# Decayed attention and a sticky mixture of experts on one core: where the transposed groups of q and k get their bank, who copies them, and the order of the last queries' value products

## The chip, the cores and the metric

The kernel runs on one core of a Trainium2 chip. The metric is the device time of one execution in microseconds. The engines are named as the profile names them: PE (TensorE, with PEld for its weight loads), DVE (VectorE), ACT (ScalarE), POOL (GpSimd) and SP (SyncE, which here only issues DMAs). PSUM is the memory that PE writes its products to; the kernel uses it in banks of 128 x 512 float32.

## The reference

q, k and v have 8 batches, 8 heads, 576 positions and 64 columns; f has a decay factor per position. Causal attention with a decay is followed by a layer of 8 experts, of which each token uses one:

```python
scores = scale * q @ k.T                       # per batch and head, 576 x 576
cum = cumsum(log(clip(f, 1e-4, 1)))
scores = where(causal, -1e9, scores + cum[:, None] - cum[None, :])
attn = softmax(scores)
x = attn @ v                                   # heads side by side: [8, 576, 512]

logits = x @ w_gate;  local = sigmoid(x @ w_local)
for s in range(576):                           # per batch, in order
    fresh = argmax(logits[s])
    e = fresh if s == 0 or local[s] < 0.5 else prev_e
    prev_e = e
    out[s] = softmax(logits[s])[e] * (relu(x[s] @ w1[e]) @ w2[e])
```

w1 is 8 x 512 x 1024 and w2 is 8 x 1024 x 512.

## The kernel before

**Number format.** Every float32 factor is split in two float16 parts, a high and a low one, and a product is made of three float16 products (high with high, high with low, low with high).

**Attention.** For each batch b there are 25 units. Twenty of them have 128 queries: per pair of heads j two "c" units, two "a" units and one "b" unit. The 576 positions leave 64 queries over, and these are the last-query units: four of them (`d1unit`, lines 958 to 995) take the last 64 queries of two heads against the first 512 keys, one head on PSUM partitions 0 to 63 and the other on 64 to 127, and a fifth (`d2unit`, lines 997 to 1006) takes them against the last 64 keys for all eight heads.

A unit goes through stages: `sc` scores into a bank "st" (PE, line 863), `mx` the negative maximum (DVE, line 874), `ex` the exponential (ACT, line 891), `tr` the transpose of the result into a bank "pt" (PE, line 906), `hi` its high part (ACT, line 911), `lo` the low part as a difference (DVE, line 915), and `av` the value products (PE, line 885) into a bank "xp". Some units take another way to the low part: `sub` subtracts on PE (line 918) and `lo2` copies on ACT (line 923). `SUBS` (line 30) lists these units. `n1` and `n2` (DVE, lines 946 and 950) divide by the sums. In `av` each block has three products: high weights with high and low values, low weights with high values. A last-query unit has 24 products with 64 stationary columns; all twelve of one half come before the twelve of the other.

**Banks.** PSUM has four banks "st", two "pt" and two "xp" (lines 115 to 117).

**q and k of the next batch.** While batch b runs, `prep(b + 1)` (line 484) hands work to POOL: high and low parts of q, then k, then v. From b = 2 on q and k are then turned (`prep_turned`, line 420) in groups of eight 128 x 128 blocks, five groups for each (the fifth has four): `tq` is eight transposes on PE (line 447) into a bank "pt", `eq` the copy out of it, on ACT for q (lines 454 and 457, with the scale) and on DVE for k (line 452). After the second, fourth and fifth group a DMA issued by SP carries the high parts to a second copy, QB or KB (lines 366 and 373), which the second half of every score needs. There are two copies of these in turn, so the next batch's can be written while the present one is read.

**Order.** The order of instructions on each engine is fixed when the program is written. A planner (`issue`, line 1204) keeps a list of units for each stage and clocks for the engines, estimates when each candidate could start, and takes the one with the lowest start plus the weight `W` of its stage; equal ones are ranked by `RANK` (lines 1125 to 1127). A stage also needs room among its banks. Groups of q and k come into the lists in `add_turns` (line 1234), as soon as POOL's part has been handed out, before each unit's `step`. Scores of the next batch wait, in the planner's reckoning, for the groups that they need (line 1115).

**Side work.** The gate of batch b - 1 and, after every second batch, the routing of two batches (which expert, which slot) are a chain of small steps that the planner mixes in as stage "side". They are put in at unit `GI` of the batch (lines 42 and 1731): 21 in batch 1, 16 in the later ones. Routing steps run on DVE and partly on POOL, those of the third pair of batches, which fall into the last batch, on DVE alone. `early_idx` and `early_tok` (lines 1699 and 1703) at the end of that chain fetch the first three tiles of expert 0's tokens from the first six batches, so that expert 0 can start as soon as the attention ends.

**Experts.** Lines 1650 and 1664 are the products of the experts; the last pair's routing runs beside the first three tiles.

Of the kernel before, what the change touches and what calls it, by code (L numbers as in the profile page):

```python
# [26 lines left out]
ROUND = 1.5 * 2.0 ** 30  # L27
CAP = 5
EARLY = 3
SUBS = (3, 5, 8, 16, 18)  # L30


def moves_of(d):
# [5 lines left out]
ORDA = moves_of("q0:P k:M 0:V 1:V k:ag")  # L39
ORDB = moves_of("q:ag q0:T 2:V q1:P k0:P k1:P q:e k:e 3:V q1:T q:Tl k0:T :vl :Vl q:2 q:C 0:K k1:T :iv v0:P k:2 1:K")  # L40

GI = (21, 16, 16)
LI = (14, 18)
PX = 6
XI = 3

UO = tuple(range(25))
NP = 0
# [15 lines left out]
def kernel(  # L64
# [355 lines left out]
    def prep_turned(b, nm):  # L420

        def begin():
            if line["eq"]:
                issue((line["eq"][-1][0], "eq"))
            new_prep(b, nm)
            prep_aug(b, nm)

        def half(g0, g1):
            R = {}

            def parts(i):
                t, t16 = LT[b, nm], Tq[b][nm + "t"]
                if not R:
                    hi, lo = (t16[:, :, 0:64], t16[:, :, 64:128]) if nm == "q" else (t16[:, :, 64:128], t16[:, :, 0:64])
                    R["p"] = hi_lo(hi[:, g0:g1], lo[:, g0:g1], t[:, g0:g1], (g1 - g0) // 2)
                R["p"][i][1]()

            return [(64 * (g1 - g0), lambda i=i: parts(i)) for i in range(3)]

        def group(j):  # L440
            U = {}

            def tq():
                t16 = Tq[b][nm + "t"]
                U["pt"] = psT.tile([128, 8, 128], F16, name="pt")
                for a in range(4 if j == 4 else 8):
                    nc.tensor.transpose(U["pt"][:, a], t16[:, 8 * j + a], ident16)  # L447

            def eq():
                A, pt = Tq[b][nm + "A"], U["pt"]  # L450
                if nm == "k":
                    nc.vector.tensor_copy(flat(A[:, 8 * j:min(8 * j + 8, 36)]), flat(pt[:, 0:4 if j == 4 else 8]))
                elif j == 4:
                    nc.scalar.activation(flat(A[:, 32:36]), flat(pt[:, 0:4]), AF.Copy, scale=SCALE)
                else:
                    dst = flat(A[:, 0:32]).rearrange("p (c g x) -> p g c x", c=2, x=64)[:, 8 * j:8 * j + 8]
                    nc.scalar.activation(dst, pt.rearrange("p g (c x) -> p g c x", c=2), AF.Copy, scale=SCALE)
                if j in (1, 3):
                    copy_hi(b, nm, 2 * j - 2, 2 * j + 2)
                elif j == 4:  # L460
                    copy_last(b, nm)

            c = 0.5 if j == 4 else 1.0
            eng, cost = ("ACT", 130 + 880 * c) if nm == "q" else ("DVE", 100 + 570 * c)
            return {"key": (b, nm, j), "tq": ("PE", 460 * c, tq, {"psT": 1}, {}), "eq": (eng, cost, eq, {}, {"psT": 1})}

        def ready(js):
            return (0, lambda: turns.extend(group(j) for j in js))

        return [(0, begin)] + half(0, 16) + [ready((0, 1))] + half(16, 36) + [ready((2, 3, 4))]  # L470
# [358 lines left out]
    def compute(b, T):  # L829
# [48 lines left out]
            nc.tensor.matmul(xo[:, :, 64], lhsT=eps[:, 0:128], rhs=eps[:, 128:128 + xo.shape[1]], start=True, stop=False,  # L878
                             skip_group_check=True)

        def av(xo, ph, pl, blks):
            n = len(blks)
            for i, (c0, m, vi) in enumerate(blks):
                for jj, (a, w) in enumerate(((ph, vh), (ph, vl), (pl, vh))):
                    nc.tensor.matmul(xo, lhsT=a[:, c0:c0 + m], rhs=w[:, vi, :],  # L885
                                     start=False, stop=(i == n - 1 and jj == 2),
                                     skip_group_check=True)

        def expo(P, st, c0, c1, bias):

# [67 lines left out]
        def d1unit(j):  # L958
            c = 32 + j

            def sc():
                if j == 0:
                    d2 = X["d2"] = psS.tile([128, 512], F32, name="st")
                    scores(d2, [(4 * r + jj, 4, (4,), r * 64, jj * 64, jj == 0) for jj in range(4) for r in range(2)])
                    for jj in range(4):
                        nc.tensor.matmul(d2[:, jj * 64:(jj + 1) * 64], lhsT=mA2, rhs=mB2,
                                         start=False, stop=True, skip_group_check=True)
                    X["P2"] = work.tile([128, 256], F32, name="P2", bufs=1)
                st = X["d", j] = psS.tile([128, 512], F32, name="st")
                scores(st, [(4 * r + j, 4, ORD4, r * 64, 0, True) for r in range(2)])  # L970

            def mx():
                if j == 0:
                    negmax(nm[:, 40:44], X["d2"][:, 0:256].rearrange("p (j x) -> p j x", j=4))
                negmax(nm[:, 44:45], X["d", j])

            def mn():
                nc.vector.tensor_tensor(nm[:, c:c + 1], nm[:, 44:45], nm[:, 40 + j:41 + j], ALU.min)

            def ex(P):  # L980
                expo(P, X["d", j], 0, 512, nm[:, c:c + 1])
                nc.scalar.activation(X["P2"][:, j * 64:(j + 1) * 64], X["d2"][:, j * 64:(j + 1) * 64], AF.Exp,
                                     bias=nm[:, c:c + 1])

            def avf(ph, pl):
                if j == 0:
                    X["xd"] = psX.tile([128, 4, 65], F32, name="xp")
                    guard(X["xd"])
                for r in range(2):
                    av(X["xd"][r * 64:(r + 1) * 64, j, :], ph, pl,  # L990
                       [(i * 128 + r * 64, 64, c * 8 + 4 * r + j) for i, c in enumerate(ORD4)])

            unit(sc, mx, ex, avf, (1020 if j == 0 else 478, 930 if j == 0 else 598, 769, 705 if j == 0 else 680), takes=1 + (j == 0),
                 frees=1 + (j == 3), first=j == 0)
            units[-1]["mn"] = "DVE", 69, mn, {}, {}

        def d2unit():
            def avf(ph, pl):
                for j in range(4):
                    g, u = j // 2, j % 2  # L1000
                    for r in range(2):
                        av(X["xd"][r * 64:(r + 1) * 64, j, :], ph, pl,
                           [(g * 128 + r * 64, 64, 32 + 4 * u + 2 * r + g)])

            unit(nop, nop, None, avf, (0, 0, 0, 680), cols=256, src=lambda: X["P2"])
            norm(lambda: X["xd"], xnl, [128, 4])

        def aunit(j, r):
# [17 lines left out]
            def avf(ph, pl):  # L1026
                if r == 0:
                    X["xp", j] = psX.tile([128, 6, 65], F32, name="xp")
                    guard(X["xp", j])
                xp = X["xp", j]  # L1030
                av(xp[:, r, :], ph, pl, [(0, 128, h)])
                av(xp[:, 4 + r, :], ph, pl, [(128 + i * 128, 128, c * 8 + h) for i, c in enumerate(ORD3)])

            unit(sc, mx, ex, avf, (545, 663, 715, 360 + 25 * (r == 0)), first=r == 0)

        def bunit(j):
# [11 lines left out]

            def avf(ph, pl):
                for r in range(2):  # L1050
                    av(X["xp", j][:, 2 + r, :], ph, pl,
                       [(r * 256 + i * 128, 128, i * 8 + 2 * j + r) for i in range(2)])

            unit(sc, mx, ex, avf, (543, 598, 716, 360))
            norm(lambda: X["xp", j].rearrange("p (c r) x -> p c r x", r=2),
# [2 lines left out]
        def cunit(j, r):  # L1058
# [13 lines left out]
            def avf(ph, pl):  # L1072
                if r == 0:
                    X["xc", j] = psX.tile([128, 2, 65], F32, name="xp")
                    guard(X["xc", j])
                av(X["xc", j][:, r, :], ph, pl, [(i * 128, 128, c * 8 + h) for i, c in enumerate(ORD4)])

            unit(sc, mx, ex, avf, (488, 598, 571, 360 + 25 * (r == 0)), first=r == 0)
            if r == 1:
# [42 lines left out]
    STAGES = ("sc", "mx", "mn", "ex", "tr", "hi", "lo", "sub", "lo2", "av", "n1", "n2", "tq", "eq")  # L1122
    RANK = {st: 0.0 for st in STAGES + ("side",)}
    RANK["side"] = -20
    RANK.update({'sc': 8.2, 'mx': 13.1, 'mn': -16.4, 'ex': 24.2, 'tr': -17.4, 'hi': 3.9, 'lo': 8.2, 'sub': -2.5, 'lo2': -6.1, 'av': 12.7, 'n1': -11.4, 'n2': -7.3, 'side': -52.7, 'tq': 30.0, 'eq': -10.0})
    W = {st: 0 for st in RANK}
    W.update({'sc': -70, 'mx': -60, 'mn': -270, 'ex': 270, 'tr': -130, 'hi': -40, 'lo': -150, 'sub': -140, 'lo2': 0, 'av': -40, 'n1': -180, 'n2': -110, 'side': -180, 'tq': 0, 'eq': -100})
    clock = {"PE": T0, "ACT": T0, "DVE": T0, "POOL": T0}
    due = deque()
    pools = {}  # L1130
# [45 lines left out]
    def side_next():  # L1176
        eng, cost = COSTS.get(chain[0].__name__, ("DVE", 160))
        after = [side["end"]]
        if chain[0].__name__ in OPENS and side["run"] is None:
            if not room["psS"]:  # L1180
                return None, eng, cost
# [49 lines left out]
    turned = {}  # L1231
    count = [0]

    def add_turns():
        while turns:
            u = turns.popleft()
            u["ready"] = clock["POOL"]
            n = serial[0] - 0.5 + 1e-4 * count[0]
            count[0] += 1
# [467 lines left out]
    for b in range(B):  # L1707
# [3 lines left out]
        for i, u in enumerate(units):  # L1711
# [4 lines left out]
            if not due:  # L1716
                if b < B - 1 or i < XP:
                    pump((23 if b == B - 1 else 25) - i)
                ship(i if i < 24 else 99)
                add_turns()  # L1720
            step(u)
            if b == B - 1:
                if i == 5:
# [3 lines left out]
                    ectx = ExitStack()  # L1727
                    ep = ectx.enter_context(tc.tile_pool(name="ep", bufs=1, side="right"))
                    W0 = wtiles(wpa)
                    queue.extend(early_weights(stage, W0, range(6)))  # L1730
            if b > 0 and i == GI[(b > 1) + (b >= B - 2)]:
                for j, x in enumerate(gate(b - 1)):
# [299 lines left out]
```

## Time and profile before

| | |
|---|---|
| median of 3 timed runs | 951.12 us (948.55 to 955.56) |
| profiled execution | 944.52 us, its span 942.8 us |
| mean granted PE clock in it | 0.965 |
| attention ends, first expert product | about 457 us, 459.48 us |
| a batch in the middle of the attention | 53 to 56 us, 25 units |
| last batch | 393 to 457 us |

A line of the profile's groups or of its order in time names the engine, the line of the kernel, the operation, the tiles out<-in with their shapes, the count and the duration; in square brackets or behind the last bar stands the idle time of the engine just before it and what ended it. A line of a stretch has its length, then the busy time of PE, PEld, DVE, ACT and POOL with the number of instructions, then the granted PE clock, the DMA engines' busy share and GB/s. An "x2" in the order of time joins two instructions that started together or one right behind the other.

### The profile page before, as it was taken

To read this page: it belongs to the slowest core of one execution; us is meant where nothing else is said; L and a number is where in the kernel's file an instruction comes from. 1 tells how busy PE (TensorE), PEld (TensorE's weight loads), DVE (VectorE), ACT (ScalarE), POOL (GpSimd) and SP (SyncE) were. 2 spreads that over 40 slices of the span, in tenths; PEclk is the share of its full clock that TensorE was granted. 3 is DMA by queue.
4 is the path that set the end of the run, shared out by engine and by line. 5 is a ranking of instruction groups with operands and counts; after the bars stand their busy time and mean duration, and the time that the engine had idled before them with its cause. 6 is when DMAs were issued, how large, how long until landed. Compare 5 with 4: busy or idle time off the path is not lost.

```text
span 942.8 us, 21055 instructions
## 1 busy us (share of the span) xinstructions
PE 832.2 (88%) x8566; PEld 571.5 (61%) x8566; DVE 530.1 (56%) x1109; ACT 425.2 (45%) x795; POOL 417.4 (44%) x479
## 2 busy tenths in 40 slices
PE   5697989889898889878886998799999999999993
PEld 3575777677776777666644664465647465655651
DVE  7584777777687767897563586433414243433200
ACT  5685868487785858566322322131312323131110
POOL 9685985395836957156632204213040312333020
PEclk9898999999999999998998999899999999999997
DMA  7989968355756644174637639936272837332010
GB/s 171 197 158 208 193 125 184 83 123 128 167 126 137 158 102 105 38 194 114 154 111 200 189 96 251 267 78 198 87 224 94 221 120 190 123 90 87 1 42 6
DMA packets 210243, 130.58 MB, mean 138 GB/s; under 512 B 149054, under 2 KB 185024, under 8 KB 210060
## 3 DMA queue, kind: packets, MB, share of 16 engines
q1 hardware_dynamic: 202369, 104.83, 48.6%
q0 software_dynamic: 7776, 24.39, 7.9%
q8 instruction: 68, 1.11, 0.5%
q14 instruction: 30, 0.25, 0.1%
HBM read 77.39 MB, written 20.41 MB: 104 GB/s over the span
## 4 chain that ended last, share of the span: by engine, by line
PE 64%; DVE 11%; DMA 9%; ACT 5%; POOL 4%; issue 4%; SPq 2%; POOLq 0%; DVEq 0%; ACTq 0%
PE z L1650 20%; PE y L1664 18%; PE pt L906 7%; PE st L863 7%; PE xp L885 6%; DVE pl L915 2%; DMA stg<-in_moe_w_dram 2%; DVE nm L874 2%; ACT P L891 2%; DMA KB<-Ak 2%; ACT ph L911 1%; DMA out_dram<-o,xs 1%; POOL xr L305 1%; PE pt L447 1%; PE st L870 1%
## 5 line engine op out<-in xcount | busy, mean ns | idle before, releaser
L1650 PE MATMUL z<-xT,wh 128*128 128x320 f16 (+3 forms) x1088 | 193.4, 298 | 18.4 <-DVE hl L1637 17.9
L891 ACT ACTIVATE P<-st,nm 128x512 f32<-128x512 f32 (+3 forms) x288 | 152.0, 584 | 60.9 <-DVE nm L874 56.5
L874 DVE TENSOR_REDUCE nm<-st 128x1 f32<-128x512 f32 (+4 forms) x264 | 133.8, 544 | 41.1 <-PE st L870 35.0
L1650 PEld LDWEIGHTS <-wh 128*128 128x128 f16 x1088 | 105.7, 99 | 61.2 <-issue 16.7
L906 PE MATMUL pt<-ident,P 128*128 128x128 f32 x784 | 123.4, 285 | 21.8 <-DVE pl L915 11.7
L911 ACT CAST ph<-pt 128x512 f16<-128x512 f32 (+1 forms) x200 | 114.5, 582 | 48.3 <-PE pt L906 43.3
L1618 POOL DMA_INDIRECT xg<-xs,mg x37 | 44.0, 1188 | 194.1 <-DMA xT<-xg 164.5
L1664 PE MATMUL y<-uh,hh 128*128 128x512 f16 x328 | 125.0, 381 | 3.7 <-ACT o L1641 3.7
L915 DVE TENSOR_TENSOR pl<-pt,ph 128x512 f16<-128x512 f32 (+1 forms) x160 | 106.5, 670 | 36.7 <-ACT ph L911 33.4
L1664 PE MATMUL y<-ul,hh 128*128 128x512 f16 x328 | 125.0, 381 | 0.0
L1664 PE MATMUL y<-uh,hl 128*128 128x512 f16 x328 | 124.8, 381 | 0.0
L1650 PE MATMUL z<-xT,wl 128*128 128x320 f16 (+3 forms) x544 | 123.7, 297 | 0.0
L1636 ACT ACTIVATE hh<-z 128x640 f16<-128x640 f32 (+3 forms) x80 | 48.4, 607 | 164.5 <-PE z L1650 155.3
L1637 DVE SCALAR_TENSOR_TENSOR hl<-z,hh 128x640 f16<-128x640 f32 (+3 forms) x80 | 55.8, 701 | 113.2 <-ACT hh L1636 113.2
L1664 PEld LDWEIGHTS <-hh 128*128 128x128 f16 x656 | 64.2, 98 | 79.3 <-issue 5.3
L906 PEld LDWEIGHTS pt<-ident,P 128*128 128x128 f32 x784 | 86.0, 144 | 34.7 <-ACT pl L923 8.4
L885 PE MATMUL xp<-VH,pl 128*128 128x65 f16 (+1 forms) x960 | 99.4, 195 | 3.1 <-DVE pl L915 1.9
L885 PE MATMUL xp<-VH,ph 128*128 128x65 f16 (+1 forms) x960 | 101.5, 198 | 0.1
L885 PE MATMUL xp<-VL,ph 128*128 128x65 f16 (+1 forms) x960 | 100.3, 196 | 0.0
L885 PEld LDWEIGHTS <-ph 128*128 128x128 f16 (+1 forms) x1920 | 91.6, 103 | 14.2 <-issue 10.3
L863 PE MATMUL st<-KB,QB 70*128 70x256 f16 (+4 forms) x448 | 81.0, 290 | 14.8 <-DMA KB<-Ak 14.8
L1642 POOL DMA_INDIRECT out_dram<-o,ms x37 | 40.1, 1085 | 109.1 <-ACT o L1641 64.9
(345 smaller groups left out, 1315.7 us busy)
## 6 DMA issues: line engine op xcount, KB each, us to landing
stg<-in_moe_w_dram SPq DMA_DIRECT2D x64, 512.0 KB
xs<-xr SPq DMA_DIRECT2D x16, 512.0 KB
ldq<-in_q_dram SPq DMA_DIRECT2D x14, 512.0 KB
ldk<-in_k_dram SPq DMA_DIRECT2D x14, 512.0 KB
ldv<-in_v_dram SPq DMA_DIRECT2D x28, 256.0 KB
KB<-Ak SPq DMA_DIRECT2D x14, 256.0 KB
QB<-Aq SPq DMA_DIRECT2D x13, 256.0 KB
ldv<-in_v_dram SPq DMA_DIRECT2D x20, 64.0 KB
```

The costliest lines, as they stand in the source:

```text
L863: nc.tensor.matmul(st[p0:p0 + m, co:co + n], lhsT=queries(lq, kk, h, c), rhs=rhs, start=(ps == 0 and first and co == col), stop=(ps == 1), ...
L874: nc.vector.tensor_reduce(dst, src, axis=AX.X, op=ALU.max, negate=True)
L885: nc.tensor.matmul(xo, lhsT=a[:, c0:c0 + m], rhs=w[:, vi, :], start=False, stop=(i == n - 1 and jj == 2), skip_group_check=True)
L891: nc.scalar.activation(P[:, c0:c1].rearrange("p (k x r) -> p k r x", r=2, x=64), st[:, c0:c1].rearrange("p (k r x) -> p k r x", r=2, x=64) ...
L906: nc.tensor.matmul(U["pt"][:, i * 128:(i + 1) * 128], lhsT=P[:, i * 128:(i + 1) * 128], rhs=ident, is_transpose=True, start=(i == 0), stop ...
L911: nc.scalar.copy(U["ph"][:, :cols], U["pt"][:, :cols])
L915: nc.vector.tensor_tensor(U["pl"][:, :cols], U["pt"][:, :cols], U["ph"][:, :cols], ALU.subtract)
L1618: nc.gpsimd.indirect_dma_start(out=xg, out_offset=None, in_=xs[0:rows], in_offset=bass.IndirectOffsetOnAxis(ap=cols(i), axis=0))
L1636: nc.scalar.activation(hv, z[:, 0:nh, 0:wd], AF.Relu)
L1637: nc.vector.scalar_tensor_tensor(lv, z[:, 0:nh, 0:wd], 0.0, hv, ALU.max, ALU.subtract)
L1650: nc.tensor.matmul(z[:, a, 0:wd], lhsT=w[:, d, fc * 128:(fc + 1) * 128], rhs=xT[:, x, a * wd:(a + 1) * wd], start=(i == 0), stop=(i == len ...
L1664: nc.tensor.matmul(y, lhsT=a[:, fc, t * 128:(t + 1) * 128], rhs=u[:, fc], start=(i == 0), stop=(i == len(prods) - 1))
```

## The change

1. The groups of q and k take a bank "st" (four of them, shared with the scores) in place of a bank "pt".
2. Copies of the groups: q's groups 0, 1, 3 and 4 go to DVE, with the scale in the instruction, and group 2 stays on ACT; k's groups 0 to 3 stay on DVE and group 4 goes to ACT (`TE`). Before, q was all on ACT and k all on DVE.
3. A group enters the planner's lists only from a given unit on (`TS`): q's at units 10, 14, 14, 17, 18, k's at 18, 20, 21, 21, 21. At the start of a batch's preparation all that are left enter at once.
4. Four units in place of five take the way through `sub` and `lo2`, and they are others (`SUBS`).
5. Gate and routing are put in at unit 20 in place of 16 from batch 2 on (`GI`), and `early_tok` is held until its pool is open.
6. `RANK` and `W` have new values.
7. `av` takes several sets of blocks and goes through them in turn: in the last-query units one product for partitions 0 to 63, then one for 64 to 127. The other units pass one set at a time, and their order stays. The planner's costs of the last-query units' products follow (705, 680, 680 become 400, 385, 385).

```diff
-SUBS = (3, 5, 8, 16, 18)
+SUBS = (7, 11, 14, 16)
-GI = (21, 16, 16)
+GI = (21, 20, 20)
+TS = {"q": (10, 14, 14, 17, 18), "k": (18, 20, 21, 21, 21)}
+TE = {"q": "DDADD", "k": "DDDDA"}
...
         def begin():
+            add_turns(99)
...
-                U["pt"] = psT.tile([128, 8, 128], F16, name="pt")
+                U["pt"] = psS.tile([128, 8, 128], F16, name="st")
...
-                if nm == "k":
-                    nc.vector.tensor_copy(flat(A[:, 8 * j:min(8 * j + 8, 36)]), flat(pt[:, 0:4 if j == 4 else 8]))
-                elif j == 4:
-                    nc.scalar.activation(flat(A[:, 32:36]), flat(pt[:, 0:4]), AF.Copy, scale=SCALE)
+                dst, src = flat(A[:, 8 * j:min(8 * j + 8, 36)]), flat(pt[:, 0:4 if j == 4 else 8])
+                if nm == "q" and j < 4:
+                    dst = flat(A[:, 0:32]).rearrange("p (c g x) -> p g c x", c=2, x=64)[:, 8 * j:8 * j + 8]
+                    src = pt.rearrange("p g (c x) -> p g c x", c=2)
+                if TE[nm][j] == "A":
+                    nc.scalar.activation(dst, src, AF.Copy, scale=SCALE if nm == "q" else 1.0)
+                elif nm == "q":
+                    nc.vector.tensor_scalar(dst, src, SCALE, None, ALU.mult)
                 else:
-                    dst = flat(A[:, 0:32]).rearrange("p (c g x) -> p g c x", c=2, x=64)[:, 8 * j:8 * j + 8]
-                    nc.scalar.activation(dst, pt.rearrange("p g (c x) -> p g c x", c=2), AF.Copy, scale=SCALE)
+                    nc.vector.tensor_copy(dst, src)
...
-            eng, cost = ("ACT", 130 + 880 * c) if nm == "q" else ("DVE", 100 + 570 * c)
-            return {"key": (b, nm, j), "tq": ("PE", 460 * c, tq, {"psT": 1}, {}), "eq": (eng, cost, eq, {}, {"psT": 1})}
+            eng, cost = ("ACT", 130 + 880 * c) if TE[nm][j] == "A" else ("DVE", 100 + 570 * c)
+            return {"key": (b, nm, j), "tq": ("PE", 460 * c, tq, {"psS": 1}, {}), "eq": (eng, cost, eq, {}, {"psS": 1})}
...
-        def av(xo, ph, pl, blks):
-            n = len(blks)
-            for i, (c0, m, vi) in enumerate(blks):
+        def av(ph, pl, *sets):
+
+            n = len(sets[0][1])
+            for i in range(n):
                 for jj, (a, w) in enumerate(((ph, vh), (ph, vl), (pl, vh))):
-                    nc.tensor.matmul(xo, lhsT=a[:, c0:c0 + m], rhs=w[:, vi, :],
-                                     start=False, stop=(i == n - 1 and jj == 2),
-                                     skip_group_check=True)
+                    for xo, blks in sets:
+                        c0, m, vi = blks[i]
+                        nc.tensor.matmul(xo, lhsT=a[:, c0:c0 + m], rhs=w[:, vi, :],
+                                         start=False, stop=(i == n - 1 and jj == 2),
+                                         skip_group_check=True)
...
-                for r in range(2):
-                    av(X["xd"][r * 64:(r + 1) * 64, j, :], ph, pl,
-                       [(i * 128 + r * 64, 64, c * 8 + 4 * r + j) for i, c in enumerate(ORD4)])
+                av(ph, pl, *((X["xd"][r * 64:(r + 1) * 64, j, :],
+                              [(i * 128 + r * 64, 64, c * 8 + 4 * r + j) for i, c in enumerate(ORD4)]) for r in range(2)))
...
-    RANK.update({'sc': 8.2, 'mx': 13.1, 'mn': -16.4, 'ex': 24.2, 'tr': -17.4, 'hi': 3.9, 'lo': 8.2, 'sub': -2.5, 'lo2': -6.1, 'av': 12.7, 'n1': -11.4, 'n2': -7.3, 'side': -52.7, 'tq': 30.0, 'eq': -10.0})
+    RANK.update({'sc': -20.2, 'mx': 39.7, 'mn': -7.5, 'ex': 80.9, 'tr': -11.9, 'hi': -3.6, 'lo': 1.1, 'sub': 15.5, 'lo2': 1.2, 'av': 12.4, 'n1': -23.3, 'n2': -3.6, 'side': -52.7, 'tq': 30.8, 'eq': -17.3})
-    W.update({'sc': -70, 'mx': -60, 'mn': -270, 'ex': 270, 'tr': -130, 'hi': -40, 'lo': -150, 'sub': -140, 'lo2': 0, 'av': -40, 'n1': -180, 'n2': -110, 'side': -180, 'tq': 0, 'eq': -100})
+    W.update({'sc': -100, 'mx': -220, 'mn': -450, 'ex': 40, 'tr': -160, 'hi': -90, 'lo': -350, 'sub': -140, 'lo2': -70, 'av': -70, 'n1': -250, 'n2': -290, 'side': -180, 'tq': -170, 'eq': -430})
...
+        if chain[0] is early_tok and "open" not in EX:
+            return None, eng, cost
...
-    def add_turns():
-        while turns:
-            u = turns.popleft()
+    def add_turns(i):
+        for u in [u for u in turns if TS[u["key"][1]][u["key"][2]] <= i]:
+            turns.remove(u)
...
+                    EX["open"] = True
```

More of the change, by code (lines that the diff above doesn't have):

```diff
@@ L988, in avf @@
                     guard(X["xd"])
-                for r in range(2):
-                    av(X["xd"][r * 64:(r + 1) * 64, j, :], ph, pl,
-                       [(i * 128 + r * 64, 64, c * 8 + 4 * r + j) for i, c in enumerate(ORD4)])
-            unit(sc, mx, ex, avf, (1020 if j == 0 else 478, 930 if j == 0 else 598, 769, 705 if j == 0 else 680), takes=1 + (j == 0),
+                av(ph, pl, *((X["xd"][r * 64:(r + 1) * 64, j, :],
+                              [(i * 128 + r * 64, 64, c * 8 + 4 * r + j) for i, c in enumerate(ORD4)]) for r in range(2)))
+            unit(sc, mx, ex, avf, (1020 if j == 0 else 478, 930 if j == 0 else 598, 769, 400 if j == 0 else 385), takes=1 + (j == 0),
                  frees=1 + (j == 3), first=j == 0)
@@ L1000, in avf @@
                     g, u = j // 2, j % 2
[L1001 to L1005, printed above, removed]
+                    av(ph, pl, *((X["xd"][r * 64:(r + 1) * 64, j, :],
+                                  [(g * 128 + r * 64, 64, 32 + 4 * u + 2 * r + g)]) for r in range(2)))
+            unit(nop, nop, None, avf, (0, 0, 0, 385), cols=256, src=lambda: X["P2"])
             norm(lambda: X["xd"], xnl, [128, 4])
@@ L1030, in avf @@
                 xp = X["xp", j]
-                av(xp[:, r, :], ph, pl, [(0, 128, h)])
-                av(xp[:, 4 + r, :], ph, pl, [(128 + i * 128, 128, c * 8 + h) for i, c in enumerate(ORD3)])
+                av(ph, pl, (xp[:, r, :], [(0, 128, h)]))
+                av(ph, pl, (xp[:, 4 + r, :], [(128 + i * 128, 128, c * 8 + h) for i, c in enumerate(ORD3)]))
             unit(sc, mx, ex, avf, (545, 663, 715, 360 + 25 * (r == 0)), first=r == 0)
@@ L1050, in avf @@
                 for r in range(2):
-                    av(X["xp", j][:, 2 + r, :], ph, pl,
-                       [(r * 256 + i * 128, 128, i * 8 + 2 * j + r) for i in range(2)])
+                    av(ph, pl, (X["xp", j][:, 2 + r, :],
+                                [(r * 256 + i * 128, 128, i * 8 + 2 * j + r) for i in range(2)]))
             unit(sc, mx, ex, avf, (543, 598, 716, 360))
@@ L1075, in avf @@
                     guard(X["xc", j])
-                av(X["xc", j][:, r, :], ph, pl, [(i * 128, 128, c * 8 + h) for i, c in enumerate(ORD4)])
+                av(ph, pl, (X["xc", j][:, r, :], [(i * 128, 128, c * 8 + h) for i, c in enumerate(ORD4)]))
             unit(sc, mx, ex, avf, (488, 598, 571, 360 + 25 * (r == 0)), first=r == 0)
@@ L1719 @@
                 ship(i if i < 24 else 99)
-                add_turns()
+                add_turns(i)
             step(u)
```

## The prediction

> **What bounds the kernel now.** I read the engine line of the page first, then the busy time by stretches of the span, then the instructions in order of time around one batch change, and last the groups of instructions that the change touches.
>
> ```profile
> span 942.8 us, 21055 instructions
> PE 832.2 (88%) x8566; PEld 571.5 (61%) x8566; DVE 530.1 (56%) x1109; ACT 425.2 (45%) x795; POOL 417.4 (44%) x479
> ```
>
> The shares mix two stages. Attention ends near 457 us, where the first expert product starts; behind that the change moves nothing but the start. So the stretches of attention alone: five whole batches with their sum, the last batch, and the ten microseconds around each batch change (first, last, and the sum of all six).
>
> ```profile
> core 0: us, PE busy (x) PEld busy (x) DVE busy (x) ACT busy (x) POOL busy (x), PEclk, DMA share, GB/s
> 121.00:175.00 54.00, 48.52 (x776) 39.21 (x776) 40.91 (x100) 39.23 (x79) 32.09 (x35) 1.00 0.62 134
> ...
> sum 272.00, PE 243.25 PEld 195.89 DVE 204.72 ACT 191.51 POOL 173.80; mean PE 48.65 PEld 39.18 DVE 40.95 ACT 38.30 POOL 34.76
> ```
> ```profile
> 393.00:457.00 64.00, 51.34 (x750) 40.89 (x750) 55.08 (x131) 38.22 (x81) 33.66 (x31) 0.92 0.48 124
> ```
> ```profile
> 121.00:131.00 10.00, 7.13 (x151) 5.96 (x152) 5.29 (x10) 2.47 (x4) 7.83 (x10) 1.00 0.35 72
> ...
> 391.00:400.00 9.00, 7.19 (x120) 5.81 (x120) 8.52 (x26) 3.70 (x8) 1.29 (x2) 1.00 0.20 44
> sum 60.00, PE 45.24 PEld 37.26 DVE 36.01 ACT 14.26 POOL 30.39; mean PE 7.54 PEld 6.21 DVE 6.00 ACT 2.38 POOL 5.07
> ```
> And the five stretches between the batch changes (first and sum):
> ```profile
> 131.00:175.00 44.00, 41.39 (x625) 33.26 (x624) 35.61 (x90) 36.76 (x75) 24.26 (x26) 1.00 0.69 148
> ...
> sum 219.00, PE 203.56 PEld 163.17 DVE 175.23 ACT 180.36 POOL 143.41; mean PE 40.71 PEld 32.63 DVE 35.05 ACT 36.07 POOL 28.68
> ```
>
> Between changes PE is busy 203.56/219 = 93% and sets the pace; DVE has 80%, ACT 82%. Around a change PE has 45.24/60 = 75% and ACT 24%: a bubble, six times. The last batch is another case: DVE 55.08/64 = 86% and PE 80%, because the routing runs on DVE there. The bubble in order of time:
>
> ```profile
> 178.52 1.06 PE L447 MATMUL pt<-ident,t16k 128*128 128x128 f16 x16
> ...
> 179.41 0.68 DVE L452 COPY Ak<-pt 128x1024 f16<-128x1024 f16 x1
> ...
> 180.15 1.77 PE L447 MATMUL pt<-ident,t16k 128*128 128x128 f16 x20 [0.56 <-DVE Ak L452]
> ...
> 183.67 0.57 PE L863 MATMUL st<-KB,QB 70*128 70x512 f16 x1 [1.54 <-DMA KB<-Ak]
> ...
> 185.18 0.71 ACT L891 ACTIVATE P<-st,nm 128x512 f32<-128x512 f32 x1 [7.75 <-DVE nm L874]
> ```
>
> All 36 transposes of the next batch's k run after the last value product; their copies and the DMA that carries half of them to KB stand in a row ahead of the next scores. Their data lay ready long before:
>
> ```profile
> 141.92 2.76 POOL L305 TENSOR_TENSOR t16k<-ldk,t16k 128x640 f16<-128x640 f32 x2
> ```
> ```profile
> 210.77 1.41 POOL L305 TENSOR_TENSOR t16k<-ldk,t16k 128x640 f16<-128x640 f32 x1
> ```
>
> That is 34 us before the change at 178.5 us in a batch without routing on POOL, and 18 us before the one at 230 us in a batch with it. The groups wait for their rank and for one of two "pt" banks, which the unit transposes always take first.
>
> **The change, part by part.** *Banks and steps.* The groups take one of four "st" banks and are let in at units 10 to 18 (q) and 18 to 21 (k). No instruction is added. Scores run ahead through the same four banks, so a group shortens that lead, which is slack as long as a scored unit waits. I expect k's groups before the batch change. The 45.24 us of PE work around the six changes, at the 93% of the other stretches, take 48.7 instead of 60 us: 11.3 us gained. Bounds: a loss of what PE would wait for a late group in mid-batch (the rival below), 0 if the groups still end up last, 14.8 us if no idle PE time is left there. With the psT banks free of groups the unit transposes can only start sooner. On SP the KB copies move ahead with their groups, past the loads of later q and k, which then wait for a DVE copy; those loads feed POOL work of the batch after, so I put this at nothing (without that cover, a copy's wait per batch, some 3 us from 180.79, below, to 183.67).
>
> ```profile
> 180.79 1.85 SPq L366 DMA_DIRECT2D KB<-Ak  x2
> ```
>
> *Alternating halves.* A last-query unit's 24 products of 64 columns, and how two units behave where the order already alternates after every three:
>
> ```profile
> 391.50 0.22 PE L885 MATMUL xp<-VH,ph 128*64 128x65 f16 x1
> 391.55 0.20 PE L885 MATMUL xp<-VL,ph 128*64 128x65 f16 x1
> ...
> 392.15 0.20 PE L885 MATMUL xp<-VH,pl 128*64 128x65 f16 x1
> ```
> ```profile
> 402.13 0.20 PE L885 MATMUL xp<-VL,ph 128*64 128x65 f16 x2
> ...
> 402.45 0.20 PE L885 MATMUL xp<-VH,pl 128*64 128x65 f16 x2
> ```
>
> One unit takes 0.65 us from first to last start. In the second fence (every row there is a x2) eleven rows lie 0.32 us apart, 32 ns for two products: the halves run side by side. Twelve pairs take 0.385 us, so 0.27 us less for each of 4 units in 8 batches: 8.6 us of PE, and 9 at 93%. [...]
>
> *Copies.* The groups concerned:
>
> ```profile
> L915 DVE TENSOR_TENSOR pl<-pt,ph 128x512 f16<-128x512 f32 x152 | 103.2, 683 | 34.9 <-ACT ph L911 31.6 <-PE xp L885 1.2 <-issue 0.5
> ...
> L452 DVE COPY Ak<-pt 128x1024 f16<-128x1024 f16 x24 | 15.9, 685 | 1.9 <-PE pt L447 1.6
> ...
> L452 DVE COPY Ak<-pt 128x512 f16<-128x512 f16 x6 | 2.5, 415 | 0.0
> ```
> ```profile
> L457 ACT ACTIVATE Aq<-pt 128x1024 f16<-128x1024 f16 x24 | 24.2, 1029 | 6.1 <-PE pt L447 5.9
> ...
> L923 ACT CAST pl<-pt 128x512 f16<-128x512 f32 x40 | 23.7, 592 | 4.7 <-PE pt L918 3.7
> ```
> ```profile
> L918 PE MATMUL pt<-ph,minus x40: 377/379/586, 29.5 to 447.0; 128*128 128x512 f16 x40
> ```
>
> Per batch DVE takes three full q groups and q's half one and loses k's half one, which cancel: +3 x 0.685 = 2.05 us. ACT loses 3 x 1.029 = 3.1 us. No row shows the scaled copy on DVE; it costs between the plain copy's 0.685 and ACT's 1.029 us, and I take the plain copy, nearest in engine and shape. [...] One subtraction unit less (SUBS 5 to 4): DVE +0.683, ACT -0.592, PE between 0 and -0.379; I take -0.25, since 32 ns for 65 columns, above, scale to 0.25 for 512.
>
> *Batch rate after.* PE: 48.65 - 1.08 - 0.25 = 47.3 us, at 93% 50.9 us. DVE: 40.95 + 2.73 = 43.7 us, and at the 86% that the last batch shows it can hold, 50.8 us. Both say 50.8 against 272/5 = 54.4: -3.6 us, five times, -18 us. DVE is then as near as PE to setting the pace.
>
> *Gate and routing at unit 20 instead of 16; weights of the list.* Four units are 4 x 54.4/25 = 8.7 us. Routing on DVE moves out of the sixth batch into the last, k's copies the other way:
>
> ```profile
> 389.07 1.04 DVE L1421 TENSOR_TENSOR_SCAN IN<-carry,OHA 128x80 f16<-128x80 f16 x1
> ...
> 390.61 0.62 DVE L1423 TENSOR_TENSOR EX<-IN,OHA 128x80 f16<-128x80 f16 x1
> ...
> 391.27 1.12 DVE L1425 TENSOR_TENSOR EX<-EX,cnt 128x80 f16<-128x80 f16 x1
> ```
> ```profile
> L452 DVE COPY Ak<-pt 128x1024 f16<-128x1024 f16 x4 | 2.7, 685 | 0.0
> ```
>
> These three make +2.8 us, SUBS +0.7, k's copies -2.7: the last batch goes from 55.1 to 55.9 us of DVE, +0.9 us at 86%. Early tokens come 8.7 us later relative to the attention:
>
> ```profile
> 435.65 4.03 SPq L1620 DMA_TRANSPOSE xT<-xg  x3
> ```
> ```profile
> 459.48 0.82 PE L1650 MATMUL z<-xT,wh 128*128 128x384 f16 x2
> ```
>
> They are ready at 439.7, used at 459.5: 19.8 us of cover, 11 left, so nothing. The guard on their step costs nothing by the same cover; the other units' value products keep their order. Batches 0 and 1 gain the halves, 2 x 1.08 = 2.2 us, against 2 x 0.683 = 1.4 us of DVE, nothing if it lies beside PE's work.
>
> **Sum.** -18 (in which the bubbles' 11.3 us and the halves stand already), - 2.2 + 1.4 for batches 0 and 1 if PE does not hide the DVE part, + 0.9 for the last batch: between -17.9 and -19.3. I take -18. The profiled execution took 944.5 us (942.8 span and 1.7 around it), so 926.5; the median of the timed runs is 6.6 us above it (951.1): 933.
>
> **The rivals.** *DVE becomes the bound, and it ends slower* (0.13). For: DVE goes to 43.7 of 50.8 us and cannot skip a late instruction. If the scaled copy costs 1.03 us, DVE has 44.7 us a batch; held to today's 80%, that is 55.9 us, +1.5 five times, and the three other batches' extra subtraction on DVE adds 3 x 0.683/0.8 = 2.6: +10, 961. Against: 86% was held in the last batch. It decides once DVE cannot pass 82%, 44.7/54.4.
>
> *k's groups are still late* (0.12). POOL's split of k, 18 us early in batches with routing on POOL, slips behind routing steps inserted later, or the list keeps the groups for the end. POOL does wait in order for such steps:
>
> ```profile
> 180.92 0.21 POOL L1447 TENSOR_TENSOR lo<-pos,t 128x10 f16<-128x10 f32 x1 [6.53 <-DVE t L1321]
> ```
>
> Two such waits would use up 13 of the 18 us. Then only the halves (9 us) and SUBS on PE (8 x 0.25 = 2 us) count, less 1 in the last batch: -10, 941.
>
> [...]
>
> *Early tokens late* (0.06): the routing chain loses its turn on DVE for more than the 11 us of cover; at 8 us beyond, 941.
>
> *More than forecast* (0.15): the unit transposes, now alone in their two banks, lift PE to 97%: 47.3/0.97 = 48.8, -5.6 five times and -4 at the ends, 919.
>
> **Numbers.** The forecast has 0.50, its own range 922 to 943. All cases together: 914 to 953, leaving out about 1 in 10 on the slow side and less below. This kernel's measurement tells about 1% from no change. Faster by over 1% (below 941.6): 0.50 x 0.9 + 0.15 + a third of the 0.22 of the three cases at 941, 0.67. Slower by over 1% (above 960.6): most of the first rival, 0.11. Same: the rest, 0.22.
>
> **What would show it.** Right: k's L447 rows before the batch's last L885 rows; no L863 row waiting for KB<-Ak; ACT's largest gap at a change well under 7.75 us; last-query L885 rows all x2, 0.36 us from first to last start; batches of 51 us with DVE at 86%. Wrong: PE rows waiting on DVE "pl" or "Ak" in mid-batch for more than the 7% of now, an L447 row waiting for POOL t16k, or the first z row waiting for xT.

## The result: 956.22 us, 0.6% slower

The changed kernel takes 956.22 us (median, 951.10 to 960.42) against 950.76 us for the kernel before, timed beside it (944.11 to 955.56). The ratio is 1.0057, with a 95% interval of 1.0038 to 1.0076. The forecast was 933 us, and the range ended at 953: the prediction was wrong.

### The profile after

The line numbers of the changed kernel lie some 10 higher: scores are L870, value products L895, unit transposes L916, the transposes of the groups L451. First the page's span and engine line:

```profile
span 953.2 us, 21059 instructions
PE 813.7 (85%) x8558; PEld 557.8 (59%) x8558; DVE 545.8 (57%) x1135; ACT 403.5 (42%) x769; POOL 416.9 (44%) x479
```

PE has 18.5 us less work than before, and the span is 10.4 us longer. The next two views tell why this is no contradiction. The stretches of the span (length, then the busy time of PE, PEld, DVE, ACT and POOL) for five batches, each from the last value product of one to that of the next:

```profile
core 0: us, PE busy (x) PEld busy (x) DVE busy (x) ACT busy (x) POOL busy (x), PEclk, DMA share, GB/s
139.70:179.00 39.30, 38.44 (x696) 32.40 (x691) 34.15 (x80) 28.99 (x63) 19.89 (x23) 1.00 0.63 144
...
sum 227.20, PE 220.61 PEld 182.40 DVE 205.68 ACT 175.73 POOL 151.28; mean PE 44.12 PEld 36.48 DVE 41.14 ACT 35.15 POOL 30.26
```

And ten microseconds that hold each of six batch changes, the first and the sum (the first change, at 139.7 us, lies at the end of its stretch; from 136 to 146 us PE is busy for 9.98 of 10):

```profile
130.00:140.00 10.00, 10.00 (x143) 8.18 (x142) 7.95 (x18) 7.02 (x16) 9.83 (x9) 0.84 1.01 180
...
sum 60.00, PE 57.41 PEld 47.03 DVE 54.88 ACT 45.14 POOL 47.60; mean PE 9.57 PEld 7.84 DVE 9.15 ACT 7.52 POOL 7.93
```

The attention became far faster than forecast: 45.4 us a batch, with PE at 97% and DVE at 91%, and the bubbles are gone (57.41 of 60 us, before 45.24). One batch change in order of time:

```profile
160.75 0.61 PE L451 MATMUL st<-ident,t16k 128*128 128x128 f16 x8
...
164.70 0.62 PE L451 MATMUL st<-ident,t16k 128*128 128x128 f16 x8
...
166.62 1.28 PE L451 MATMUL st<-ident,t16k 128*128 128x128 f16 x20
...
175.82 0.38 PE L870 MATMUL st<-KB,QB 70*128 70x512 f16 x1
...
177.86 0.22 PE L895 MATMUL xp<-VH,ph 128*64 128x65 f16 x2
...
178.23 0.20 PE L895 MATMUL xp<-VH,pl 128*64 128x65 f16 x2
...
178.99 0.21 PE L895 MATMUL xp<-VH,pl 128*64 128x65 f16 x2
```

All 36 transposes of k are done 11 us before the last value product (178.99), and scores of the next batch, which need KB, start at 175.8, ahead of it and without a wait. A last-query unit's products are pairs (twelve rows of x2 from 177.86 on), 0.37 us from first to last start.

The attention's last value product comes at 406.1 us, where it came at 459.3 before. Then the gain is lost:

```profile
core 0: us, PE busy (x) PEld busy (x) DVE busy (x) ACT busy (x) POOL busy (x), PEclk, DMA share, GB/s
406.10:420.00 13.90, 1.52 (x19) 0.63 (x13) 6.03 (x17) 0.77 (x2) 10.99 (x12) 0.63 0.90 236
420.00:467.00 47.00, 6.09 (x53) 4.06 (x53) 18.80 (x78) 0.90 (x3) 16.64 (x27) 0.50 0.15 34
```

For 60.9 us PE does 7.6 us of work. In order of time, PE's long waits in that stretch:

```profile
426.10 0.22 PE L1442 MATMUL st<-EX,ones 128*128 128x80 f16 x1 [10.04 <-POOL EX L1435]
431.78 0.83 PE L1485 MATMUL st<-RH,LO 128*128 128x80 f16 x10 [5.46 <-POOL RH L1478]
437.18 1.16 PE L1535 MATMUL st<-rp,LO 128*128 128x120 f16 x10 [4.58 <-POOL rp L1529]
...
449.88 0.84 PE L1485 MATMUL st<-RH,LO 128*128 128x80 f16 x10 [4.76 <-DVE LO L1479]
454.50 1.16 PE L1535 MATMUL st<-rp,LO 128*128 128x120 f16 x10 [3.77 <-DVE rp L1529]
455.59 0.16 PE L1544 MATMUL st<-ones,cnt 128*1 128x1 f16 x1
466.99 0.48 PE L1660 MATMUL z<-xT,wh 128*128 128x384 f16 x1 [11.24 <-DMA xT<-xg]
```

These are the second routing (its first product on PE at 406.2) and the third, one behind the other, with no attention left beside them, and after them the fetch of the early tokens. The longest wait within a routing, 10.04 us, has its own cause: the second routing's step EX runs on POOL, its input was ready at 416.1, and until 425.3 POOL was preparing expert weights. The first expert product (z) starts at 466.99, 7.5 us later than before; the other 2.9 us of the 10.4 lie behind it. A first z row that waits for xT was among the prediction's signs of being wrong. Two lines bracket a routing: `rows` (its first product on PE, before L1361, now L1371) and `pinvert` (its last ten, L1525, now L1535). The kernel before, then the changed one (first and last of three routings):

```profile
L1361 PE MATMUL st<-order,kp x3: 222/222/222, 162.7 to 380.7; 128*10 128x128 f16 x3
...
L1525 PE MATMUL st<-rp,LO x30: 212/216/216, 223.5 to 421.1; 128*128 128x120 f16 x30
```
```profile
L1371 PE MATMUL st<-order,kp x3: 222/223/270, 208.4 to 439.0; 128*10 128x128 f16 x3
...
L1535 PE MATMUL st<-rp,LO x30: 213/304/308, 397.7 to 455.4; 128*128 128x120 f16 x30
```

Before, the first routing came to pinvert at 223.5 us, 61 us after rows. Now it begins 46 us later and needs 189 us, to 397.7. The third has all its steps on DVE: it took 40 us before (380.7 to 421.1) and takes 16 with nothing beside it (439.0 to 455.4); the second, partly on POOL, takes 31 (406.2 to 437.2). It isn't the steps that take long, but the time between them. Two steps of the first routing that follow each other, on DVE in order of time:

```profile
192.37 0.23 DVE L1359 TENSOR_REDUCE F<-eq 128x10 f32<-128x80 f32 x1
192.96 0.69 DVE L462 TENSOR_SCALAR Aq<-st 128x1024 f16<-128x1024 f16 x1 [0.36 <-PE st L451]
193.57 0.68 DVE L925 TENSOR_TENSOR pl<-pt,ph 128x512 f16<-128x512 f32 x1
194.16 1.01 DVE L462 TENSOR_SCALAR Aq<-st 128x1024 f16<-128x1024 f16 x2
195.19 0.69 DVE L925 TENSOR_TENSOR pl<-pt,ph 128x512 f16<-128x512 f32 x1
195.80 2.54 DVE L881 TENSOR_REDUCE nm<-st 128x1 f32<-128x128 f32 x5
198.25 0.18 DVE L956 RECIPROCAL rs<-xp 128x6 f32<-128x6 f32 x1
198.36 0.13 DVE L1363 TENSOR_TENSOR G<-is__182,kp 128x20 f16<-128x20 f16 x1
```

Between them eleven instructions of the attention went ahead: group copies (`eq`, weight -430), low parts (`lo`, -350), a maximum (`mx`, -220), a reciprocal (`n1`, -250). The weight of "side", -180, is the old one, and of two candidates that could start together the lower weight goes first. Before, side steps stood ahead of `mx` (-60), `eq` (-100), `n2` (-110) and `lo` (-150) and level with `n1` (-180); only `mn` (-270, the smaller of two maxima) went ahead of them. Now all six stages that run on DVE stand ahead, and DVE is 91% busy.

### The profile page after: what moved, and what is told of

Same layout as the page of the kernel before. It is cut to its first block, busy times and chain, and to the rows that moved or that the text cites. A ratio compares the mean times of both kernels' runs of the same rounds, so it can differ in the third digit from the quotient of the medians.

```text
span 953.2 us, 21059 instructions
## 1 busy us (share of the span) xinstructions
PE 813.7 (85%) x8558; PEld 557.8 (59%) x8558; DVE 545.8 (57%) x1135; ACT 403.5 (42%) x769; POOL 416.9 (44%) x479
## 5 line engine op out<-in xcount | busy, mean ns | idle before, releaser
L916 PE MATMUL pt<-ident,P 128*128 128x128 f32 x784 | 121.3, 283 | 10.4 <-DVE pl L925 5.8
L925 DVE TENSOR_TENSOR pl<-pt,ph 128x512 f16<-128x512 f32 x168 | 111.0, 674 | 28.6 <-ACT ph L921 20.5
L916 PEld LDWEIGHTS pt<-ident,P 128*128 128x128 f32 x784 | 84.7, 143 | 24.3 <-DVE pl L925 7.8
L895 PE MATMUL xp<-VH,ph 128*128 128x65 f16 (+1 forms) x960 | 90.3, 197 | 0.0
L895 PE MATMUL xp<-VL,ph 128*128 128x65 f16 (+1 forms) x960 | 89.1, 195 | 0.0
L895 PE MATMUL xp<-VH,pl 128*128 128x65 f16 (+1 forms) x960 | 88.5, 194 | 0.2
L870 PE MATMUL st<-KB,QB 70*128 70x256 f16 (+4 forms) x448 | 79.5, 288 | 9.8 <-DMA KB<-Ak 6.4
L895 PEld LDWEIGHTS <-ph 128*128 128x128 f16 (+1 forms) x1920 | 80.9, 102 | 9.1 <-issue 5.3
```

What stands on the lines that cost most here:

```text
L870: nc.tensor.matmul(st[p0:p0 + m, co:co + n], lhsT=queries(lq, kk, h, c), rhs=rhs, start=(ps == 0 and first and co == col), stop=(ps == 1), ...
L916: nc.tensor.matmul(U["pt"][:, i * 128:(i + 1) * 128], lhsT=P[:, i * 128:(i + 1) * 128], rhs=ident, is_transpose=True, start=(i == 0), stop ...
L925: nc.vector.tensor_tensor(U["pl"][:, :cols], U["pt"][:, :cols], U["ph"][:, :cols], ALU.subtract)
```

## The experiments

The theory from here on: **the new list weights put the six DVE stages of the attention ahead of the side steps, so the routings come late, and two of them run alone.** Rivals: the later unit of gate and routing (GI) does it; or another part of the change costs the time and the late routing is only its sign. Ratios are to the kernel before, run on the same chip; where two experiments are compared in us, it is the difference of their ratios times 950 us, unless medians are named.

### e1 and e8: side steps first again

```diff
-'n1': -250, 'n2': -290, 'side': -180, 'tq': -170, 'eq': -430   # W of the changed kernel
+'n1': -250, 'n2': -290, 'side': -460, 'tq': -170, 'eq': -430   # e1;  -300 in e8
```

> Theory S: in the changed kernel the routing steps lose their turn on DVE, because the list's new weights put the maxima (-220), low parts (-350), divisions (-250, -290) and copies (-430) ahead of a side step (-180); the chain of three routings piles up and two of them run alone behind the attention. With the side weight at -460, below all DVE stages, and nothing else changed, the hole from about 406 to 467 us goes, the first expert product starts a few us behind the last value product, and the attention ends at 420 to 435 us, since the routing's DVE work comes back into it: 905 to 930 us, ratio 0.95 to 0.98. Rivals G (routing put in four units later), P (side steps find no st bank, which the groups now take) and E (the guard on the early tokens' step): the side weight alone changes little, the hole stays, 945 to 960 us.

> The side weight at -300, behind low parts, copies and the small minimum on DVE, ahead of maxima and divisions. Theory S: each routing takes longer than with -460 but ends before the next begins; the third ends nearer to the attention's end, still ahead of it. The attention ends a few us earlier, as fewer waits are put into it: 922 to 932 us. If the third chain runs over the attention's end, 935 or more and a hole ahead of the first expert product.

Measured: e1 930.43 us, 0.9805 (0.9758 to 0.9853); e8 927.92 us, 0.9764 (0.9724 to 0.9804). One number takes 24 us off the changed kernel (1.0057 less 0.9805). The two routing lines and the first expert product in e1:

```profile
L1371 PE MATMUL st<-order,kp x3: 216/222/222, 173.0 to 372.8; 128*10 128x128 f16 x3
...
L1535 PE MATMUL st<-rp,LO x30: 216/216/308, 226.6 to 406.2; 128*128 128x120 f16 x30
```
```profile
440.99 0.20 PE L895 MATMUL xp<-VH,pl 128*64 128x65 f16 x2
441.13 0.50 PE L1660 MATMUL z<-xT,wh 128*128 128x384 f16 x2
```

The first routing takes 54 us again, the last ends 35 us before the attention does, and z follows the last value product by 0.14 us. The attention ends at 441.0 and not at 406.1: the routing's work now lies beside it. So of the 61 us behind the attention in the changed kernel 35 are time that the attention had been spared, and 26 are what it cost to do the routing last. At -300 the side steps stand ahead of `mx`, `n1` and `n2` only, and that is enough.

### e3: the same fault put into the kernel before

```diff
-'n1': -180, 'n2': -110, 'side': -180, 'tq': 0, 'eq': -100   # W of the kernel before
+'n1': -180, 'n2': -110, 'side': -20, 'tq': 0, 'eq': -100
```

> The kernel before with one number changed, the side weight from -180 to -20, which is above all its DVE weights. Theory S: the same hole appears without any of the change's other parts: the attention ends some 5 to 15 us earlier, then routing steps run alone for some 20 to 30 us, PE at its half clock for part of it: 955 to 975 us. Rivals G, P and E: without the later unit, the shared banks and the guard nothing piles up: 945 to 955 us.

Measured: 964.64 us, 1.0178 (1.0129 to 1.0227). Routing and the first z:

```profile
L1361 PE MATMUL st<-order,kp x3: 222/222/222, 176.5 to 436.9; 128*10 128x128 f16 x3
...
L1525 PE MATMUL st<-rp,LO x30: 215/217/305, 281.6 to 467.6; 128*128 128x120 f16 x30
```
```profile
479.82 0.80 PE L1650 MATMUL z<-xT,wh 128*128 128x384 f16 x2 [11.86 <-DMA xT<-xg]
```

The same picture without any other part of the change: the attention ends sooner (443.4 us against 459.3), the third routing begins 6.5 us before its end in place of 79 us (380.7), and z is late, at 479.8. From 443.4 to 480 us PE works for 3.44 us, at a granted clock of 0.53. The order of the list alone makes it.

### e2: the old unit for gate and routing

```diff
-GI = (21, 20, 20)
+GI = (21, 16, 16)
```

> The changed kernel with gate and routing put in at unit 16 again, and nothing else. Theory S: the chain starts 9 us earlier and still starves, so most of the hole stays: 940 to 957 us. Rival G: four units were what pushed the chain behind the attention, and the hole goes: 905 to 930 us.

Measured: 962.58 us, 1.0166 (1.0113 to 1.0218), above both ranges that were expected and 10 us slower than the changed kernel; what costs these 10 us was not tried. In order of time on PE:

```profile
431.98 0.23 PE L1442 MATMUL st<-EX,ones 128*128 128x80 f16 x1 [14.68 <-POOL EX L1435]
...
472.76 0.80 PE L1660 MATMUL z<-xT,wh 128*128 128x384 f16 x2 [11.20 <-DMA xT<-xg]
```

Put in four units sooner, the routing still comes behind the attention. The rival falls.

### e5: all old weights, everything else new

```diff
-    RANK.update({'sc': -20.2, 'mx': 39.7, ...})   # RANK and W of the changed kernel
-    W.update({'sc': -100, 'mx': -220, ...})
+    RANK.update({'sc': 8.2, 'mx': 13.1, ...})     # both as in the kernel before
+    W.update({'sc': -70, 'mx': -60, ...})
```

> The changed kernel with the stages' ranks and weights of the kernel before; banks, copies, steps of the groups, SUBS, gate unit and alternating halves as changed. Theory S: a side step (-180) again goes ahead of maxima (-60), low parts (-150) and copies (-100), so no routing is left behind the attention, and the rest of the change shows its gain: 922 to 938 us, ratio 0.972 to 0.988. If the gain of the attention came from the new weights themselves, 940 to 950.

Measured: 922.09 us, 0.9727 (0.9684 to 0.9770). Five batches, and the first z:

```profile
128.40:375.00 246.60, 231.22 (x3757) 188.67 (x3752) 219.60 (x520) 175.75 (x371) 167.64 (x187) 0.98 0.68 138
```
```profile
433.75 0.50 PE L1660 MATMUL z<-xT,wh 128*128 128x384 f16 x2
```

All other parts of the change together gain 2.7%, and the new `W` and `RANK` lose 3.3% (1.0057 less 0.9727: 31 us, of which e1 gets 24 back with the weight of "side" alone; z is 33.2 us sooner here than in the changed kernel). A batch takes 49.3 us with PE at 94% and DVE at 89%.

### e9 to e12 and e4, e6, e7: the parts one by one

All of e9 to e12 start from e5; e6 and e7 start from e1; e4 starts from the kernel before.

```diff
 # e9 (from e5), e7 (from e1): groups in the old bank
-U["pt"] = psS.tile([128, 8, 128], F16, name="st")
+U["pt"] = psT.tile([128, 8, 128], F16, name="pt")
 # e10 (from e5): old copies
-TE = {"q": "DDADD", "k": "DDDDA"}
+TE = {"q": "AAAAA", "k": "DDDDD"}
 # e11 (from e5), e6 (from e1): one half after the other
-            for i in range(n):
-                for jj, (a, w) in enumerate(((ph, vh), (ph, vl), (pl, vh))):
-                    for xo, blks in sets:
+            for xo, blks in sets:
+                for i in range(n):
+                    for jj, (a, w) in enumerate(((ph, vh), (ph, vl), (pl, vh))):
 # e12 (from e5): groups enter the lists at once
-TS = {"q": (10, 14, 14, 17, 18), "k": (18, 20, 21, 21, 21)}
+TS = {"q": (0, 0, 0, 0, 0), "k": (0, 0, 0, 0, 0)}
 # e4 (from the kernel before): the last-query units' products alternate, with the planner's old costs
-                for r in range(2):
-                    av(X["xd"][r * 64:(r + 1) * 64, j, :], ph, pl, [...])
+                av2(ph, pl, *((X["xd"][r * 64:(r + 1) * 64, j, :], [...]) for r in range(2)))
```

> The kernel with the old weights (922 us, ratio 0.973) and the groups of q and k in the two pt banks again. There the groups have their old low preference, and unit transposes take the pt banks first. If the prediction's step holds, that a group without an st bank ends up behind the last value product, the bubbles come back: 11 us by the prediction's term, up to the whole gain less the halves, 933 to 945 us, and the k transposes stand again behind the last-query products. If the banks matter as little as with the new weights, 920 to 926.

> The kernel of the side weight -460 with the groups of q and k in the two pt banks again, with the same steps, copies and weights. If the banks are what lets k's groups run ahead of the batch change, the bubbles come back and 8 to 15 us are lost: 938 to 946 us. If letting them in at given units with a better weight is enough, 928 to 934.

> The kernel with the old weights, with q's copies all on ACT and k's all on DVE as before. If DVE sets the pace now, taking 2.05 us of copies a batch off it gains, 915 to 920 us. If the long ACT copies (1.03 us against 0.69) held up exponentials and high parts, 924 to 930. No difference: 920 to 924.

> The kernel with the old weights, with the last-query products in the old order. With the 0.5% that the halves gave alone in the kernel before: 925 to 929 us. If they give nothing once DVE is the busiest engine: 920 to 924.

> The kernel of the side weight -460 with the last-query products in the old order, twelve of one half before twelve of the other; the order of all else is the same. With the halves worth what they gave alone in the kernel before (0.5%), 934 to 937 us, ratio 0.984 to 0.988; with the 9 us of the prediction 939 to 941; if DVE sets the pace here and PE has room, 930 to 932.

> The kernel before with the last-query products alternating between the halves, the planner's costs and so the order of all else as before. The prediction gave this part 8.6 us of PE time, 9 us on the clock: 939 to 945 us, and every row of these products joined in pairs. [...] If PE is not what sets the pace in these units, the products get shorter and the time stays: 947 to 951 with rows in pairs.

> The kernel with the old weights, with the groups let into the lists as soon as POOL's part is handed out, as before, in place of fixed units. If the st banks alone let the groups run early, nothing is lost: 915 to 924 us. If the fixed units matter, because early groups stand in PE's queue ahead of their data or take st banks from scores: 926 to 938.

| | median, us | ratio (95% interval) | against its base | so the part is worth |
|---|---|---|---|---|
| e5 | 922.09 | 0.9727 (0.9684 to 0.9770) | | |
| e9, old bank | 944.12 | 0.9951 (0.9919 to 0.9982) | e5 | bank: 21 us |
| e10, old copies | 927.45 | 0.9793 (0.9742 to 0.9844) | e5 | copies: 6 us |
| e11, halves in a row | 929.82 | 0.9802 (0.9760 to 0.9845) | e5 | halves: 7 us |
| e12, no fixed units | 913.47 | 0.9632 (0.9584 to 0.9680) | e5 | fixed units: -9 us |
| e4, halves alone | 943.85 | 0.9947 (0.9917 to 0.9978) | before | halves: 5 us |
| e6, halves in a row | 928.27 | 0.9783 (0.9749 to 0.9816) | e1 | halves: -2 us, not told from 0 |
| e7, old bank | 929.74 | 0.9796 (0.9758 to 0.9834) | e1 | bank: -1 us, not told from 0 |

The intervals of e10 and e11 overlap that of e5, and that of e12 just misses it: these worths of 6 to 9 us are uncertain by some 6. e6 and e12 came out faster than any of the ranges expected of them.

The bank is worth 21 us with the old weights and nothing with the new ones and side steps first. The row of k's transposes at the change near 178 us, in e9 and in e7, points to why:

```profile
L451 PE MATMUL pt<-ident,t16k x36: 217/219/230, 179.4 to 183.4; 128*128 128x128 f16 x36
```
```profile
L451 PE MATMUL pt<-ident,t16k x36: 219/219/231, 158.2 to 162.5; 128*128 128x128 f16 x36
```

The last value products of that batch run from 177.2 to 180.5 us in e9 and from 172.7 to 180.6 in e7. In e9 all 36 transposes still come at the end; in e7, in the same old bank, they run 10 us ahead of those products. The two differ in all weights and ranks; that it is `tq`, -170 in place of 0, that gives the groups their turn at a "pt" bank is likely but not shown. So it is k's turn that counts, and either the bank or the new weights give it. Neither was tried alone on the kernel before.

The halves save PE time. The value products alone in the same stretch, busy PE time in e5 and in e11:

```profile
128.40:375.00 246.60, 63.02 (x1809) 54.16 (x1804) 0.98 0.68 138
```
```profile
128.40:375.00 246.60, 69.07 (x1814) 59.99 (x1808) 0.99 0.68 138
```

That is 6.05 us in five batches, 1.2 us each. Whether the end moves by as much depends on the rest: by 7 us in e11, by none in e6. Why not in e6 is open; e1's executions had a mean granted PE clock of 0.948 to 0.955 and those of e6 0.959 to 0.962, so the clock may have taken back what the halves gave.

**The best version is e12**: 913.47 us, 3.7% faster than the kernel before. It is the changed kernel with the old weights and without the fixed units.

## Why the prediction was wrong

**The step that failed** is the last part, "gate and routing at unit 20; weights of the list". It priced two things: work that moves from one batch to the next (+0.9 us) and the early tokens, "19.8 us of cover, 11 left, so nothing". It counted the 8.7 us of the later unit against that cover. The new weights, which stood in the diff, it never set against the weight of "side", and so put them at nothing without a reason. That was the part with the largest effect: 31 us (e5 against the changed kernel). The third routing ended 34 us later than before (455.4 for 421.1), and the attention that was to cover it ended 53 us sooner. A hint stood in the profile of before: the third routing took 40 us from rows to pinvert there, and the changed kernel shows that the same steps take 16 alone. A chain that its neighbours stretch to more than twice its length is one whose rank matters. The outcome, within 1% of no change, had a chance of 0.22 in the prediction.

**The rival** "early tokens late" named this mechanism, "the routing chain loses its turn on DVE", and gave it 0.06 and 941 us. The price was small because it took one routing to be late by 8 us. In fact three piled up: the first came to pinvert at 397.7, the second and the third followed it, and these ran at the pace of their own waits and, for 9 us, of POOL's expert weights. The rival "DVE becomes the bound", with 0.13 and 961, has the right size and the wrong cause: DVE held 89% to 91%.

**Bubbles and banks.** Right in direction, and k's groups went ahead of the change as expected: PE's share there rose from 45.24 to 57.41 of 60 us. That the bank does it holds with the old weights only (e9, against e7). The term was 11.3 us (bounds 0 to 14.8); e9 says 21. The bound counted only the ten microseconds around each change. Five batches of e9, in the old bank:

```profile
135.50:401.60 266.10, 238.60 (x3731) 189.90 (x3726) 214.39 (x515) 175.84 (x371) 164.15 (x184) 0.97 0.61 128
```

PE is idle for 27.5 us there, and for 15.4 in e5's five: 12 us less idle time is the term as I saw it, and about as large as I took it. Another 7 us of the difference are PE's busy time, and what makes those isn't settled. The two profiles are of the slowest execution of e9 (952.12 us) and the fastest of e5 (918.84), so the split is rough.

**Alternating halves.** Right in the mechanism and in PE's time: 0.37 us from first to last start against the 0.36 that the prediction gave among its signs, 1.2 us of PE a batch against 1.08. Of the time they gave less, 5 to 7 us against 8.6 to 9, in e4 and e11 (none in e6). Of the three cases that the prediction counts at 941, one (0.04) is that the halves do not run side by side even in turn: no run shows that, and the trace of the changed kernel has 24 starts in 0.37 us (from 177.86), 16 ns each on average.

**Copies.** The scaled copy took 0.684 us on DVE (18 of 128x1024), as the plain one (0.688); the lower bound, which I took, was right. With the old copies e10 loses 6 us, uncertain by as much; the sum had no gain of its own for them.

**Banks "let in at" fixed units.** I took that as free. Without it e12 is 9 us faster than e5.

**Batch rate.** Forecast 50.8 us with PE at 93% and DVE at 86%; e5, which has all but the weights, shows 49.3 with 94% and 89%, and ends at 922 us against the forecast's 933 (and 919 of "more than forecast"). Without the weights the forecast would have held, at the fast end of its own range (922 to 943), and partly by luck: the bank gave 21 us for 11.3, the halves 7 for 9, the copies 6 for none, and the fixed units took 9. The 86% was no limit, only the highest share that the kernel before had shown.

## What to carry to other kernels

A change to the weights of a list scheduler is priced as any other: write the new order of the stages on each engine, find who has lost rank, and follow that work to its deadline. Work off the critical path with slack at its end (a chain of many small steps above all) is the first to starve when its neighbours are put ahead, and it is only seen when nothing is left to hide it. When several parts change at once, the one with no instructions in it can outweigh all the others.

## What the runs showed of the hardware that was not expected

- Products into partitions 0 to 63 and into 64 to 127 run side by side: in the changed kernel pairs of 64-column products start together (twelve rows of x2 from 177.86), and 24 of them need 0.37 us from first to last start, where one half after the other took 0.65 in the kernel before.
- PE's granted clock falls to 0.50 while PE has only the routing's work (6.09 us of it in 420 to 467 us, above), and comes back about 4 us after the first z (0.50 in the stretch from 469 to 471 us, 0.97 from 471 to 473). The same product before and behind that point:

```profile
467.58 0.52 PE L1660 MATMUL z<-xT,wl 128*128 128x384 f16 x1
...
471.50 0.33 PE L1660 MATMUL z<-xT,wl 128*128 128x384 f16 x1
```

- One and the same small DVE instruction took 0.13 us and 1.00 us in one execution: L1363 (128x20) took 0.13 at 198.36 (above), in the middle of the attention, and 1.00 in the next routing, on a DVE that is busy for 6.03 of 13.90 us (above):

```profile
409.26 1.00 DVE L1363 TENSOR_TENSOR G<-is__182,kp 128x20 f16<-128x20 f16 x1
```

  The long row ends (410.26) as a POOL instruction ends that began before it (408.99 to 410.24). So does a row of L1397, 1.08 us from 412.76, with POOL's work to 413.81; with POOL idle the two take 0.16 and 0.17 us (439.55, 441.90). The prediction priced three routing steps by rows of before (2.8 us), and two of those, at 389.07 and 391.27, also end within 0.2 us of a POOL instruction's end. It looks as if such a row waits for POOL, but this was not tried.
